# A gated mix of a 2-D spectral filter and a diagonal state space layer: the recurrence re-ordered with chunks outermost, loads released in steps, small work moved between engines

## Chip, cores and metric

The kernel runs on one core of a Trainium2 chip. The metric is device time of one execution in microseconds; the median of three runs of the kernel before is 387.51 us (385.86 to 391.31). Engines are named as in the profile: PE (matmul), PEld (its weight loads), DVE (vector), ACT (scalar), POOL (GpSimd) and SP, which here only issues DMAs. A name with q, such as SPq, is the engine's instruction queue.

## What is computed

`x` has 2048 rows (time) and 1024 columns. Two results are mixed per row by a gate:

```python
X = rfft2(x)                                   # 2048 x 513, complex
a = irfft2(X * (w_r + 1j * w_i)).bfloat16

Lam_bar = exp(exp(log_dt) * Lam)               # 1024 complex states
Bu = einsum("bld,pd->blp", x, B_bar)
h  = Lam_bar * h + Bu[:, t]                    # for each t of 2048
b  = 2 * einsum("blp,dp->bld", h, C).real + x * Dskip

g = sigmoid((x * gate_w).sum(-1))
out = g * a + (1 - g) * b
```

## The kernel before

**Layout.** `big` (16 rows of 1024 per partition) holds the Fourier coefficients, named `FX` with eight planes q, and later a part of C. `xT` is x transposed, `BT` is B transposed in eight blocks jb of 128 states, each with a real and an imaginary half; the three are filled by transposing DMAs that SP issues (L212, L217, L615). `hp` is a pool of eight tiles for h.

**First stage.** x arrives in eight loads `xt`. `fstage` forms sums and differences `eo` on DVE (four elements of each on POOL, L384 to L387), PE transforms them along time (`ps_f`, L398, L399), ACT copies each `ps_f` into two planes of FX (L403). ACT and DVE also work out the small per-state vectors (`scr`, `rho`, `beta`).

**Spectral branch** (`fft_main`). For each of 16 groups g of frequencies: `fd` (PE `ps_d`, ACT copy `X1`, L462), `bf_w` (PE `ps_xe` and `ps_xo`, ACT copies to `X`, then four DVE steps `Y`, `t` that multiply by the weights W, L487 to L490), `bi` (PE `ps_q`, ACT copy back into FX, L514). The matrices `MM` and the weights W are loaded by POOL, two or three groups ahead of need. After group 15 `Gi_sb` is loaded, and for each pair of time residues `idm` (PE `ps_id`, ACT copy `yp`), DVE's `pm` (L582, L583) and `fi` (PE `ps_y`, ACT copies `ya`) follow; SP stores `ya` in DRAM (`ya_scratch`). All `ps_` tiles of this branch share two PSUM buffers.

**State space branch** (`ssm_pair`). The 2048 time steps form four chunks c of 512, the eight state blocks four pairs q; one call does one (c, q), so there are 16, called pairs below. PE makes Bu of the two blocks (`psu`, 32 matmuls of 512 columns, L336), ACT scales it into `u` (L340). DVE rotates it with the tables `tab` (cu, su, cu: L347 to L349, each a pass over 2048 elements), runs four scans (L353), works out the carry into the next chunk in three small steps (L360 to L364), and rotates back into `h` (L367 to L369). `tables(q)` fills the tables of a pair: two ACT passes `xa`, three DVE passes, three ACT sines. `u` has two buffers, so the copy of a pair waits for the pair before the last one to be finished.

**Output** (`gate_pair`, `tile_out`). For each of 16 row tiles tb of 128, DVE multiplies x by the gate weights (`pr`, L672), ACT sums it (L673) and forms the gate `gb`; three small steps (L678 to L682) turn it into the factors `gf` and `om`. DVE scales x by Dskip (L674), ACT scales the stored spectral row (L686). PE forms `psy` (two halves of 17 matmuls: 16 of h with C, L698, and one that adds x, L701), and DVE's `o` (L705) mixes both; SP stores it. `psy` has two buffers.

**Order.** The code is written as generators that are stepped against each other; each yields an estimate of its PE time. SP and POOL keep the order of the program up to the output stage; elsewhere a scheduler places instructions by its own estimates, and the resulting order is fixed before the kernel runs: an engine works its queue in that order and waits where data is missing. The spectral branch runs against `ssm_first` (chunks 0 and 1, with q outermost: both chunks of a pair q one after the other) in the ratio 80 to 58. C arrives in two halves, the first into the first two chunks of xT (L615 by `load_C(0)`), the second into rows 0 to 7 of big (`load_C(1)`). The rows 8 to 15 of big then hold `xc` and `gac` of four row tiles. Chunk 2 runs against the output of chunk 0, with h in a pool of its own (`h2`), chunk 3 against that of chunk 1.

Of the kernel before, what the change touches and what calls it, by code (L numbers as in the profile page):

```python
# [11 lines left out]
ALU = mybir.AluOpType  # L12
# [8 lines left out]
D = 1024  # L21
# [24 lines left out]
def _host_consts():  # L46
# [38 lines left out]
    for b in range(2):  # L85
        kr = 2 * (d + P * b)[:, None]
        ki = kr + 2
        kod = kr + 1
        ck = np.where(kr == 0, 1.0, 2.0)
        Gi[:, 2 * b, 0] = (-ck * np.cos(2 * np.pi * kr * 256 / D))[:, 0]  # L90
        Gi[:, 2 * b, 1:257] = ck * np.cos(2 * np.pi * kr * n0 / D)
        ei = np.zeros((P, 512))
        ei[:, :255] = -2 * np.sin(2 * np.pi * ki * n1[:, :255] / D)
        if b == 1:
            ei[127, :] = 0
            ei[127, 255] = -1.0
            ei[127, 256:] = (-1.0) ** np.arange(256)
        Gi[:, 2 * b + 1, :] = ei
        Gi[:, 4 + 2 * b, :256] = 2 * np.cos(2 * np.pi * kod * n0 / D)
        Gi[:, 5 + 2 * b, :256] = -2 * np.sin(2 * np.pi * kod * n1 / D)  # L100
# [28 lines left out]
GW = [(0, 257), (258, 512), (770, 257), (1028, 255), (1284, 256), (1540, 256), (1796, 256), (2052, 256)]  # L129
GIW = [(0, 257), (258, 255), (514, 257), (772, 512), (1284, 256), (1540, 256), (1796, 256), (2052, 256)]  # L130
GN = 2308
# [10 lines left out]
def kernel(  # L142
# [24 lines left out]
    cG = nc.inline_tensor(_pack(hc["G"], GW), name="c_G").ap()  # L167
    cGi = nc.inline_tensor(_pack(hc["Gi"], GIW), name="c_Gi").ap()
    cMM = nc.inline_tensor(hc["MM"], name="c_MM").ap()
# [158 lines left out]

    def ssm_pair(c, q, hpool):
        u = up.tile([P, 2, 2, TC], BF16, name="u", tag="u")  # L330
# [26 lines left out]
        if c + 1 < NCH:  # L357
            ge = su[:, :, :, TC - 1]
            k1 = sm.tile([P, 2, 2], FP32, name="k1")
            nc.vector.tensor_mul(out=k1, in0=ge, in1=cTC[:, 2 * q:2 * q + 2].unsqueeze(2).to_broadcast([P, 2, 2]))  # L360
            k2 = sm.tile([P, 2, 2], FP32, name="k2")
            nc.vector.tensor_mul(out=k2, in0=ge[:, :, ::-1], in1=sg[:, 2 * q:2 * q + 2, :])
            cy = sm.tile([P, 2, 2], FP32, name=f"carry{q}")
            nc.vector.tensor_add(out=cy, in0=k1, in1=k2)  # L364
            carry[q] = cy
        h = hpool.tile(full, BF16, name="h", tag="h")
        nc.vector.tensor_mul(out=cu, in0=su, in1=tq[:, :, 0:1, ::-1].to_broadcast(full))  # L367
# [8 lines left out]
    def fstage(jj):  # L376
# [15 lines left out]
        for eo_i in range(2):  # L392
            for b in range(2):
                ps = psF.tile([P, 4, 2, P], FP32, name="ps_f", tag="ps")
                bs = slice(P * b, P * (b + 1))
                for jl in range(4):
                    v = eos[jj - 1 + jl // 2][:, jl % 2, eo_i]
                    nc.tensor.matmul(ps[:, jl], lhsT=v[:, 0, bs], rhs=FW_sb[:, 0:2 * P], start=True, stop=False)  # L398
                    nc.tensor.matmul(ps[:, jl], lhsT=v[:, 1, bs], rhs=FW_sb[:, P * (1 + eo_i):P * (3 + eo_i)],  # L399
                                     start=False, stop=True)  # L400
                q = 4 * eo_i + 2 * b
                for r in range(2):
                    nc.scalar.copy(out=FX[:, q + r, :, j0:j0 + 4], in_=ps[:, :, r, :].rearrange("p j c -> p c j"))  # L403
                yield 1.0
# [40 lines left out]
    def fd(g):  # L445
# [16 lines left out]
        nc.scalar.copy(out=X1, in_=ps)  # L462
        X1s[g] = X1

    def bf_w(g):
# [29 lines left out]
    def bi(g):  # L495
        Y = Ys.pop(g)
        M = MM.pop(g)
        Mf = M.rearrange("p a b -> p (a b)")
        nr_, r_, i_, ri_ = Mf[:, 384:512], Mf[:, 512:640], Mf[:, 640:768], Mf[:, 512:768]
        nri = Mf[:, 384:640]  # L500
        ps = psF.tile([P, 8, P], FP32, name="ps_q", tag="ps")
        Yr, Yi = Y[:, 0, :], Y[:, 1, :]
        for b in range(2):
            e = 256 * b
            nc.tensor.matmul(ps[:, 2 * b, :], lhsT=Yr[:, e:e + 255:2], rhs=r_, start=True, stop=False)
            nc.tensor.matmul(ps[:, 2 * b, :], lhsT=Yi[:, e:e + 255:2], rhs=nr_, start=False, stop=True)
            nc.tensor.matmul(ps[:, 2 * b + 1, :], lhsT=Yr[:, e + 2:e + 257:2], rhs=i_, start=True, stop=False)
            nc.tensor.matmul(ps[:, 2 * b + 1, :], lhsT=Yi[:, e + 2:e + 257:2], rhs=r_, start=False, stop=True)
        for b in range(2):
            e = 256 * b + 1  # L510
            dst = ps[:, 4 + 2 * b:6 + 2 * b, :]
            nc.tensor.matmul(dst, lhsT=Yr[:, e:e + 255:2], rhs=ri_, start=True, stop=False)
            nc.tensor.matmul(dst, lhsT=Yi[:, e:e + 255:2], rhs=nri, start=False, stop=True)  # L513
        nc.scalar.copy(out=FX[:, :, 8 * g:8 * g + 8, :], in_=ps.rearrange("p q (c j) -> p q c j", j=16))  # L514

    def idm(j, yp):
        ps = psF.tile([P, 1024], FP32, name="ps_id", tag="ps")

        def mm(q, lo, w, start, stop):
            o, n = GIW[q]  # L520
            nc.tensor.matmul(ps[:, lo:lo + w], lhsT=FX[:, q, :, j], rhs=Gi_sb[:, o:o + w],  # L521
                             start=start, stop=stop, skip_group_check=True)

        mm(3, 0, 512, True, False)
        mm(1, 0, 255, False, False)
        mm(0, 255, 257, False, False)
# [62 lines left out]


    load_BT(0)
    load_xT(0)
    load_BT(1)
    for jj in range(8):
        for _ in fstage(jj):
            pass
        if jj == 5:
            start_consts()
            load_M(0)
            load_W(0)  # L600
    tables(0)
    load_M(1)
    load_W(1)
    load_M(2)
    load_xT(1)
    for jb in range(2, 8):
        load_BT(jb)

    CH = [xT[:, :, 0:1024].rearrange("p j (r d) -> p j r d", r=2), big[:, 0:8].rearrange("p j (r d) -> p j r d", r=2)]

    def load_C(half):
        for dd in range(2):
            for ri, src in enumerate((B_C_re, B_C_im)):
                r0 = 512 * half + 256 * dd
                nc.sync.dma_start_transpose(out=CH[half][:, :, ri, 256 * dd:256 * (dd + 1)], in_=src[r0:r0 + 256, :])  # L615
        nc.vector.tensor_scalar_mul(out=CH[half][:, :, 1, :], in0=CH[half][:, :, 1, :], scalar1=-1.0)

    def ssm_first():
        for q in range(4):
            if q:  # L620
                tables(q)
            for c in range(2):
                yield from ssm_pair(c, q, hp)
            if q == 1:
                load_xT(2)
            if q == 3:
                load_xT(3)
        load_C(0)

# [16 lines left out]

    merge(Gen(fft_main()), Gen(ssm_first()), 80.0, 58.0)
    order1.close()
    fctx.close()

    with ExitStack() as bctx:
        h2 = bctx.enter_context(tc.tile_pool(name="h2", bufs=4))
        fin1 = bctx.enter_context(tc.tile_pool(name="fin1", bufs=1))
        fin = bctx.enter_context(tc.tile_pool(name="fin", bufs=2))
        psY = bctx.enter_context(tc.tile_pool(name="psY", bufs=2, space=PSUM))
        load_C(1)
        gw_bc = fin1.tile([P, D], BF16, name="gw_bc")
# [3 lines left out]

        gates = {}

        def gate_pair(tp):
            gl = fin.tile([P, 2], FP32, name="gl")
            for i in range(2):
                tb = 2 * tp + i
                xc, gac = big[:, 8 + tb % 4, :], big[:, 12 + tb % 4, :]
                nc.sync.dma_start(out=xc, in_=x[P * tb:P * (tb + 1), :])
# [7 lines left out]
            gf = fin.tile([P, 2], FP32, name="gf")  # L677
            nc.vector.tensor_copy(out=gf, in_=gb)  # L678
            ob = fin.tile([P, 2], BF16, name="ob")
            nc.vector.tensor_scalar(out=ob, in0=gb, scalar1=-1.0, scalar2=1.0, op0=ALU.mult, op1=ALU.add)  # L680
            om = fin.tile([P, 2], FP32, name="om")
            nc.vector.tensor_copy(out=om, in_=ob)  # L682
            for i in range(2):
                tb = 2 * tp + i
                gac = big[:, 12 + tb % 4, :]
                nc.scalar.activation(out=gac, in_=gac, func=ACT.Copy, scale=gf[:, i:i + 1])  # L686
                gates[tb] = om[:, i:i + 1]

        def tile_out(tb):
            c, tq = tb // 4, tb % 4  # L690
            xc, gac, om = big[:, 8 + tb % 4, :], big[:, 12 + tb % 4, :], gates[tb]
            psy = psY.tile([P, D], FP32, name="psy")
            for dh in range(2):
                ds = slice(512 * dh, 512 * (dh + 1))
                i = 0
                for jb in range(8):
                    for ri in range(2):
                        nc.tensor.matmul(psy[:, ds], lhsT=hs[c, jb // 2][:, jb % 2, ri, P * tq:P * (tq + 1)],  # L698
                                         rhs=CH[dh][:, jb, ri, :], start=(i == 0), stop=False)
                        i += 1  # L700
# [14 lines left out]

        def b_gen(c, hpool):
            for q in range(4):
                yield from ssm_pair(c, q, hpool)

        def run(g):  # L720
            for _ in g:
                pass

        gate_pair(0)
        bg = Gen(b_gen(2, h2))
        for _ in range(4):
            bg.step()
        merge(Gen(c_gen(0)), bg, 29.0, 24.0)
        merge(Gen(c_gen(1)), Gen(b_gen(3, hp)), 29.0, 29.0)
        run(c_gen(2))  # L730
        run(c_gen(3))


# [28 lines left out]
```

## Time and profile before

| | us |
|---|---|
| median of three runs | 387.51 |
| the profiled execution | 387.79 |
| its span | 386.0 |
| busy: PE, DVE, ACT, POOL | 334.1, 299.0, 197.4, 54.9 |
| all of L353 (64 scans) on DVE | 76.8 |
| all six passes L347 to L349 and L367 to L369 on DVE | 117.0 |
| mean granted PE clock | 0.973 |

The profile is one execution. Its span is the time between the first and the last instruction; 1.8 us of the execution lie outside. Durations of neighbouring instructions overlap by some 0.08 us on DVE and more on PE, since they are pipelined, so a chain of them is best summed by the distance from start to start. A wait is named by what ended it.

### The profile page before, as it was taken

Reading aid. Unit: us, or ns where it says so; the run is one execution under the profiler, and the core shown is the slowest. Engines: PE = TensorE matmul, PEld = TensorE weight load, DVE = VectorE, ACT = ScalarE, POOL = GpSimd, SP = SyncE. Lnnn points to the kernel's source line nnn. Section 1 sums busy time; section 2 is a strip of 40 time slices with the busy share of each in tenths; the row PEclk is TensorE's granted clock in tenths of the full one; section 3 lists DMA queues with packets and bytes.
Section 4 is the critical chain, followed back from the end, with each engine's and each line's share of the span. In section 5 each row is a group of like instructions: output and inputs, shape, how many; then the busy total and the mean of one; then the engine's idle time right before and its main releaser. Section 6 shows DMA issues by size and latency. Waiting matters only on the chain.

```text
span 386.0 us, 4922 instructions
## 1 busy us (share of the span) xinstructions
PE 334.1 (87%) x1794; PEld 176.3 (46%) x1827; DVE 299.0 (77%) x434; ACT 197.4 (51%) x265; POOL 54.9 (14%) x129
## 2 busy tenths in 40 slices
PE   2678969989998897989798389999999997699995
PEld 1554636536554555656343134444444443244442
DVE  3932498999999999986959499399898988984121
ACT  1999846847886767979342077333203132242200
POOL 3680423152534200000000100000000000000000
PEclk9999989989999999999989879999999998999999
DMA  8999993122313110223999704220102022054001
GB/s 302 274 281 226 176 232 83 48 68 73 95 54 91 53 43 19 110 109 101 216 225 226 269 27 139 80 82 16 68 27 82 2 82 82 2 163 136 29 28 53
DMA packets 64520, 43.17 MB, mean 112 GB/s; under 512 B 52928, under 2 KB 53088, under 8 KB 64496
## 3 DMA queue, kind: packets, MB, share of 16 engines
q1 hardware_dynamic: 60544, 33.56, 34.5%
q0 software_dynamic: 3616, 9.13, 8.8%
q8 instruction: 14, 0.23, 0.3%
q10 hardware_dynamic: 336, 0.17, 0.1%
q14 instruction: 10, 0.08, 0.1%
HBM read 21.87 MB, written 8.39 MB: 78 GB/s over the span
## 4 chain that ended last, share of the span: by engine, by line
DVE 43%; PE 25%; ACT 8%; issue 8%; DMA 8%; SPq 6%; POOL 1%; DVEq 0%; ACTq 0%
PE psy L698 16%; DVE su L353 13%; SPq L615 5%; DVE cu L347 3%; DVE su L348 3%; PE psu L336 3%; DVE cu L349 3%; DVE u L368 3%; DMA xt<-in_A_x_dram 3%; DMA MM<-c_MM 3%; DVE o L705 2%; DVE cu L367 2%; ACT u L340 2%; DVE t L488 2%; DMA gw_bc<-in_gate_w_dram 2%
## 5 line engine op out<-in xcount | busy, mean ns | idle before, releaser
L336 PE MATMUL psu<-xT,BT 128*128 128x512 bf16 x490 | 123.0, 387 | 1.2 <-issue 0.2
L698 PEld LDWEIGHTS <-h 128*128 128x128 bf16 x512 | 50.9, 99 | 78.1 <-issue 18.5
L336 PEld LDWEIGHTS <-BT 128*128 128x128 bf16 x512 | 51.0, 100 | 53.1 <-issue 5.5
L698 PE MATMUL psy<-xT,h 128*128 128x512 bf16 x252 | 59.0, 386 | 7.5 <-DVE o L705 5.7
L698 PE MATMUL psy<-big,h 128*128 128x512 bf16 x250 | 58.6, 385 | 0.5 <-issue 0.2
L353 DVE TENSOR_TENSOR_SCAN su<-r_sb,carry,cu 128x512 bf16<-128x512 f32 x48 | 58.1, 1265 | 0.1
L673 ACT ACTIVATE pr<-pr 128x1024 bf16<-128x1024 bf16 x16 | 16.9, 1054 | 80.5 <-DVE pr L672 66.3
L340 ACT ACTIVATE u<-psu,rho 128x1024 bf16<-128x1024 f32 x32 | 35.5, 1112 | 24.9 <-PE psu L336 24.9
L705 DVE SCALAR_TENSOR_TENSOR o<-psy,om,big 128x1024 bf16<-128x1024 f32 x16 | 20.4, 1278 | 24.0 <-PE psy L701 17.9
L347 DVE TENSOR_TENSOR cu<-u,tab 128x2048 bf16<-128x2048 bf16 x16 | 19.5, 1221 | 20.1 <-ACT u L340 20.1
L686 ACT ACTIVATE big<-big,gf 128x1024 bf16<-128x1024 bf16 x16 | 17.5, 1140 | 12.1 <-DVE gf L678 12.1
L398 PE MATMUL ps_f<-BT,eo 128*128 128x256 bf16 x64 | 15.9, 287 | 5.4 <-ACT big L403 5.2
L450 PE MATMUL ps_d<-G_sb,big 128*128 128x256 bf16 (+3 forms) x128 | 19.7, 293 | 0.3
L349 DVE TENSOR_TENSOR cu<-cu,su 128x2048 bf16<-128x2048 bf16 x16 | 19.5, 1221 | 0.3
L514 ACT CAST big<-ps_q 128x1024 bf16<-128x1024 f32 x16 | 16.2, 1012 | 6.9 <-PE ps_q L513 6.8
L369 DVE TENSOR_TENSOR h<-cu,u 128x2048 bf16<-128x2048 bf16 x16 | 19.5, 1218 | 0.2
L367 DVE TENSOR_TENSOR cu<-su,tab 128x2048 bf16<-128x2048 bf16 x16 | 19.5, 1218 | 0.1
L348 DVE TENSOR_TENSOR su<-u,tab 128x2048 bf16<-128x2048 bf16 x16 | 19.5, 1217 | 0.0
L368 DVE TENSOR_TENSOR u<-su,tab 128x2048 bf16<-128x2048 bf16 x16 | 19.5, 1216 | 0.0
L353 DVE TENSOR_TENSOR_SCAN su<-r_sb,cu 128x512 bf16<-128x512 f32 x16 | 18.7, 1209 | 0.1
L487 DVE TENSOR_TENSOR Y<-X,W 128x1028 bf16<-128x1028 bf16 x16 | 10.9, 681 | 9.8 <-ACT X L483 9.8
L521 PE MATMUL ps_id<-Gi_sb,big 128*128 128x256 bf16 (+3 forms) x128 | 17.6, 286 | 0.9 <-DMA Gi_sb<-c_Gi 0.9
(159 smaller groups left out, 495.7 us busy)
## 6 DMA issues: line engine op xcount, KB each, us to landing
xt<-in_A_x_dram SPq DMA_DIRECT2D x8, 512.0 KB, 5.4
ya_scratch<-ya SPq DMA_DIRECT2D x16, 256.0 KB, 2.0
big<-in_A_x_dram SPq DMA_DIRECT2D x16, 256.0 KB, 2.9
big<-ya_scratch SPq DMA_DIRECT2D x16, 256.0 KB, 2.8
out_dram<-o SPq DMA_DIRECT2D x16, 256.0 KB, 2.0
MM<-c_MM POOLq DMA_DIRECT2D x16, 192.0 KB, 2.8
W<-in_A_w_r_dram POOLq DMA_DIRECT2D x31, 64.1 KB, 2.2
W<-in_A_w_i_dram POOLq DMA_DIRECT2D x31, 64.1 KB, 2.2
```

What stands on the lines that cost most here:

```text
L336: nc.tensor.matmul(psu[:, ri, :], lhsT=BT[:, jb, ri, dblk, :], rhs=xT[:, dblk, TC * c:TC * (c + 1)], start=(dblk == 0), stop=(dblk == 7))
L340: nc.scalar.activation(out=u[:, jj], in_=psu, func=ACT.Copy, scale=rho[:, jb:jb + 1])
L347: nc.vector.tensor_mul(out=cu, in0=u, in1=tq[:, :, 0:1, :].to_broadcast(full))
L348: nc.vector.tensor_mul(out=su, in0=u[:, :, ::-1, :], in1=tq[:, :, 1:3, :])
L349: nc.vector.tensor_add(out=cu, in0=cu, in1=su)
L353: nc.vector.tensor_tensor_scan(out=su[:, jj, ri, :], data0=r_sb[:, jb:jb + 1].to_broadcast([P, TC]), data1=cu[:, jj, ri, :], initial=(0.0 ...
L367: nc.vector.tensor_mul(out=cu, in0=su, in1=tq[:, :, 0:1, ::-1].to_broadcast(full))
L368: nc.vector.tensor_mul(out=u, in0=su[:, :, ::-1, :], in1=tq[:, :, 1:3, ::-1])
L369: nc.vector.tensor_add(out=h, in0=cu, in1=u)
L450: nc.tensor.matmul(ps[:, lo:lo + w], lhsT=FX[:, q, 8 * g:8 * g + 8, :], rhs=G_sb[:, o:o + w], start=start, stop=stop, skip_group_check=True)
L698: nc.tensor.matmul(psy[:, ds], lhsT=hs[c, jb // 2][:, jb % 2, ri, P * tq:P * (tq + 1)], rhs=CH[dh][:, jb, ri, :], start=(i == 0), stop=False)
L705: nc.vector.scalar_tensor_tensor(out=o, in0=psy, scalar=om, in1=gac, op0=ALU.mult, op1=ALU.add)
```

## The change

The diff, cut to its core. Line numbers in the prediction are those of the kernel before.

```diff
-        ki = kr + 2
+        ki = kr
...
-        if b == 1:
-            ei[127, :] = 0
-            ei[127, 255] = -1.0
-            ei[127, 256:] = (-1.0) ** np.arange(256)
+        if b == 0:
+            ei[0, :] = 0
+            ei[0, 255] = -1.0
+            ei[0, 256:] = (-1.0) ** np.arange(256)
...
+    def h_tile(c, q):
+        if c != 2:
+            return hp.tile([P, 2, 2, TC], BF16, name="h", tag="h")
+        a, s = 4 * (q % 2), TC * (q // 2)
+        return xT[:, a:a + 4, s:s + TC].rearrange("p (j r) t -> p j r t", r=2)
...
-            nc.vector.tensor_mul(out=k1, in0=ge, in1=cTC[:, 2 * q:2 * q + 2].unsqueeze(2).to_broadcast([P, 2, 2]))
+            nc.gpsimd.tensor_mul(out=k1, in0=ge, in1=cTC[:, 2 * q:2 * q + 2].unsqueeze(2).to_broadcast([P, 2, 2]))
...
-            nc.vector.tensor_mul(out=k2, in0=ge[:, :, ::-1], in1=sg[:, 2 * q:2 * q + 2, :])
+            nc.gpsimd.tensor_mul(out=k2, in0=ge[:, :, ::-1], in1=sg[:, 2 * q:2 * q + 2, :])
...
-            nc.vector.tensor_add(out=cy, in0=k1, in1=k2)
+            nc.gpsimd.tensor_add(out=cy, in0=k1, in1=k2)
...
-                for r in range(2):
-                    nc.scalar.copy(out=FX[:, q + r, :, j0:j0 + 4], in_=ps[:, :, r, :].rearrange("p j c -> p c j"))
+                nc.scalar.copy(out=FX[:, q, :, j0:j0 + 4], in_=ps[:, :, 0, :].rearrange("p j c -> p c j"))
+                nc.vector.tensor_copy(out=FX[:, q + 1, :, j0:j0 + 4], in_=ps[:, :, 1, :].rearrange("p j c -> p c j"))
...
         X1s[g] = X1
+        loads_at(g, X1)
...
-        for b in range(2):
-            e = 256 * b
...
-        for b in range(2):
-            e = 256 * b + 1
...
+        for par in range(2):
+            for b in range(2):
+                e = 256 * b + par
+                dst = ps[:, 4 * par + 2 * b:4 * par + 2 * b + 2, :]
+                nc.tensor.matmul(dst, lhsT=Yr[:, e:e + 255:2], rhs=ri_, start=True, stop=False, **kw)
+                nc.tensor.matmul(dst, lhsT=Yi[:, e:e + 255:2], rhs=nri, start=False, stop=True, **kw)
+        nc.tensor.matmul(ps[0:1, 1, :], lhsT=Yr[:, 512:513], rhs=i_, start=True, stop=False, **kw)
+        nc.tensor.matmul(ps[0:1, 1, :], lhsT=Yi[:, 512:513], rhs=r_, start=False, stop=True, **kw)
...
+    def hold(dst, src):
+        nc.gpsimd.tensor_copy(out=dst, in_=src)
...
-    load_xT(1)
-    for jb in range(2, 8):
-        load_BT(jb)
...
+    def loads_at(g, X1):
+        el = X1[:, 0:1]
+        if g in (0, 2, 4):
+            for jb in (g + 2, g + 3):
+                hold(BT[:, jb, 0, 0, 0:1], el)
+                load_BT(jb)
+        elif g in (5, 11, 14):
+            c = {5: 1, 11: 2, 14: 3}[g]
+            hold(xT[:, 0, TC * c:TC * c + 1], el)
+            load_xT(c)
+    CT = big.rearrange("p (j r) d -> p j r d", r=2)
+    def load_C():
+        for qd in range(4):
+            ds = slice(256 * qd, 256 * (qd + 1))
+            for ri, src in enumerate((B_C_re, B_C_im)):
+                nc.sync.dma_start_transpose(out=CT[:, :, ri, ds], in_=src[ds, :])
+            nc.vector.tensor_scalar_mul(out=CT[:, :, 1, ds], in0=CT[:, :, 1, ds], scalar1=-1.0)
+    def ssm_all():
+        for c in range(NCH):
+            for q in range(4):
+                if c == 0:
+                    tables(q)
+                yield from ssm_pair(c, q)
...
-    merge(Gen(fft_main()), Gen(ssm_first()), 80.0, 58.0)
+    ssm = Gen(ssm_all())
+    fft = Gen(fft_main())
+    while not fft.done:
+        if ssm.t * 80.0 <= fft.t * 46.0:
+            ssm.step()
+        else:
+            fft.step()
...
-                xc, gac = big[:, 8 + tb % 4, :], big[:, 12 + tb % 4, :]
+                xc = fin.tile([P, D], BF16, name="xc", bufs=4)
+                gac = fin.tile([P, D], BF16, name="gac", bufs=4)
...
-            nc.vector.tensor_copy(out=gf, in_=gb)
+            nc.gpsimd.tensor_copy(out=gf, in_=gb)
...
-        bg = Gen(b_gen(2, h2))
-        for _ in range(4):
-            bg.step()
-        merge(Gen(c_gen(0)), bg, 29.0, 24.0)
-        merge(Gen(c_gen(1)), Gen(b_gen(3, hp)), 29.0, 29.0)
-        run(c_gen(2))
-        run(c_gen(3))
+        cg = [Gen(c_gen(c)) for c in range(NCH)]
+        while ssm.t < 8 * 7.2 + 0.0:
+            ssm.step()
+        for c in range(NCH):
+            t0 = ssm.t
+            while not cg[c].done:
+                if not ssm.done and (ssm.t - t0) * 29.0 <= cg[c].t * 29.0:
+                    ssm.step()
+                else:
+                    cg[c].step()
```

In words: all four q of a chunk come before the next chunk, and the spectral branch runs ahead, with fewer pairs beside it (80 to 46). The transposing loads of BT from block 2 on and of xT from chunk 1 on are not issued at once; `loads_at` lets them go at certain groups: POOL copies one element of X1 into the destination, and the load, which overwrites that element, has to wait for it. C is loaded in four quarters of columns into all of big. The h of chunk 2 lies in the columns of xT that held chunks 0 and 1. The odd planes of FX that belong to even frequencies use frequency k instead of k+2, so that the two halves share one 256-column right side; the frequency 512 that is left is computed by two matmuls on one column. The three steps of the carry and the three steps after the gate (`gf`, `ob`, `om`) go to POOL; the second of each two copies of `ps_f` goes to DVE. `xc` and `gac` get four buffers of their own.

## Prediction

> **What bounds the kernel now.** I read the profiled execution (387.79 us, of which 386.0 are span and 1.8 lie around it; the median of the three runs is 387.51, so the sum below also holds for the median within 0.3 us) in this order: busy time by stage, DVE's waits, the timeline of one late pair of state blocks, the timeline of the first stage.
>
> The view of busy time by window, cut at five points: the first DVE step of the recurrence (48.35), the last Y of the frequency stage (141.6), the last ps_id matmul (183.1), the end of the output step o of tile 8 (337.3), the end. Columns: window, its length, then busy us and instructions of PE, PEld, DVE, ACT, POOL, granted clock, DMA share, GB/s.
> ```profile
> 0.00:48.35 48.35, 33.93 (x232) 22.64 (x236) 21.90 (x84) 37.57 (x61) 22.44 (x66) 1.00 1.08 252
> 48.35:141.60 93.25, 82.12 (x541) 48.78 (x549) 91.06 (x129) 65.02 (x77) 30.88 (x60) 0.96 0.35 83
> 141.60:183.10 41.50, 37.97 (x228) 24.47 (x232) 36.29 (x46) 34.62 (x47) 0.54 (x1) 1.00 0.25 87
> 183.10:337.30 154.20, 136.19 (x598) 60.55 (x608) 131.51 (x156) 50.79 (x68) 1.07 (x2) 0.96 0.40 102
> 337.30:386.00 48.70, 43.95 (x200) 19.82 (x203) 18.21 (x24) 9.38 (x14) 0.00 (x0) 1.00 0.24 81
> ```
> I call them A to E. A is ACT's (37.57 busy, without a break from 10 us on). B and most of D are DVE's: 91 of 93 and 131.5 of 154 us. C is shared: ACT 34.6 of 41.5, DVE 36.3. E is pure PE: 200 matmuls that cannot start before o of tile 8 frees its psy buffer. So the end is o(8) plus 48.7 us, and o(8) is where DVE's queue says it is.
>
> DVE's 22 us of idle time in D are listed by the view of waits (who waited for whom, total, times, longest):
> ```profile
> DVE cu L347 <- ACT u L340: 14.7, 6, 4.4
> DVE pr L672 <- DMA gw_bc<-in_gate_w_dram: 4.9, 1, 4.9
> DVE pr L672 <- DMA big<-in_A_x_dram: 1.4, 1, 1.4
> ```
> The first row comes from ACT's order, as the timeline of one pair shows (start, length, engine and line):
> ```profile
> 289.92 1.23 DVE L369 TENSOR_TENSOR h<-cu,u 128x2048 bf16<-128x2048 bf16 x1
> 291.06 1.28 DVE L705 SCALAR_TENSOR_TENSOR o<-psy,om,big 128x1024 bf16<-128x1024 f32 x1
> 292.26 0.68 DVE L672 TENSOR_TENSOR pr<-big,gw_bc 128x1024 bf16<-128x1024 bf16 x1
> 292.97 0.69 DVE L674 TENSOR_TENSOR big<-big,dsk_bc 128x1024 bf16<-128x1024 bf16 x1
> 295.21 1.22 DVE L347 TENSOR_TENSOR cu<-u,tab 128x2048 bf16<-128x2048 bf16 x1 [1.55 <-ACT u L340]
> ```
> ACT's sum over pr waits for DVE's pr, and u of the next pair stands behind it on ACT, so DVE waits 1.5 us for u. One pair (cu, su, cu, four scans, cu, u, h) takes 279.03 to 291.06, 12.03 us; o takes 1.2 more, pr and xc 0.7 each.
>
> **The change, stage by stage.** PE's matmuls for Bu and for the output, and the DVE passes of 16 pairs, stay as they are in number. What moves is how many pairs lie before the last ps_id: in the built order the changed kernel has issued 232 of the 512 psu matmuls by then, the old one 260. On DVE that is 6 pairs and the start of a seventh, against 7 and the start of an eighth.
>
> Stage A. FX's evacuation is halved: 16 of 32 ACT copies of 0.53 us (6.42 us for 12) leave ACT, 8.3 us. They become 16 DVE copies from PSUM of 512 elements; the nearest row is L705, 1.28 us for 1024, so 0.62 to 0.65 each, 10 us. DVE needs, from the arrival of vps at 7.3 us: 30 eo steps spaced 0.36 (10.8), 42 small steps (3.9, the rest of 7.3 to 23.6 less its 1.6 of waits), 10 of copies, 2.5 of xa: 34.5 to 36 us. Old ACT released the first X1 at 37.7. So ACT's 8 us turn into a DVE bound about as late; but the first pair's psu is complete earlier in PE's order (ahead of the first ps_q instead of two groups later), and u of its second half stands before that ps_q copy on ACT. I take 46.0 for the first cu, from 44 (ACT's gain half kept) to 51 (DVE copies at the whole 1.28).
>
> In A too: the BT transposes past block 1 and chunk 1 to 3 of xT now wait on SP for POOL copies that wait for X1 of groups 0, 2, 4, 5, 11, 14. Queued behind them on SP are only other transposes and, much later, the ya stores; on POOL the W and MM loads. Each W load stands behind a Y step that comes later than that X1, so nothing on POOL is late by it. BT 2 and 3 are let go at 37.7; four issues of 1.31 us and 5.5 us of landing bring them by 49, and PE's order first reads them (33rd psu) at about 44, block 2's first half only, landed by then. Cost 0, at most 3 us of PE in B, where DVE has 16 us of Y and pair 1 ahead of it. What it can win: MM of group 3 landed 7.26 us after its issue at 47.08, against a median of 2.8, while the old BT and xT transposes ran; but DVE idled only 2.1 and 1.9 us in B, so the gain is 0 to 4. I take none.
>
> Stage B. Between first cu and last Y the new DVE order holds 26 passes of 2048, 16 scans, 3 table sets and the Y work, the old one 31, 20, 2 and 5 carries. At the spacing of this stage (1.135 a pass, 1.14 to 1.19 a scan, 2.35 a table set, 0.08 a small step) that is 5.7 + 5.0 + 1.2 - 2.4 = 9.5 less; 0.6 of Y comes in. 91.3 becomes 82.4. Idle: old 4, new 5.6, since the second table set puts three ACT passes of 1.05 before the u that pair 2 needs. B = 88. ACT carries about 80 us in it, 56 for the FFT copies.
>
> The k=512 edit lies here: ps_q took eight matmuls of 128 columns spaced 0.055 and four of 256 spaced 0.11, 0.88 us; now eight of 256 and two of 128, 0.99. 16 x 0.11 = 1.8 us of PE, covered by PE's wait for Y (5.5 us before ps_q in all); uncovered it costs 1.8.
>
> Stage C. Gi lands 4.5 us after the last Y and eight double steps follow. Old: ps_y on PE waited three times for DVE's pm, which stood between the passes of pairs 6 to 8; 5.1 us a step. New: DVE has 28 us of work here, so ACT paces: two yp of 1.0, four ya of 0.5, a third of a u, 4.4 us; six steps at 4.6 instead of 5.1. C = 38.5, taken 38 (35 to 41.5).
>
> Stage D. Against the old 154.2: one pair more, 12.0; o(8) now stands behind the last pair's cu, u, h, 3.5; carry and gate steps leave DVE, 30 x 0.08 = 2.3; the old idle 22 goes. New idle: C's eight transposes all start after the last ps_id (2.3 to 2.7 us each on SP, the old ones did so from 185.9 on as well), with ya stores between them; the sign flips stand in DVE's queue between pair 8's steps, and by 2.5 us a transpose and 5 of landing DVE waits 2.2, 0.9 and 0.5 for them. PE meanwhile has 39 psu and a half tile. After each pr, ACT still holds up u: with sum 1.15, u 1.0, and for every second pair gb and two gate passes (2.2), against h and xc (1.75) or cu, u, xc, h (4.1) of cover on DVE, it comes to 1.1, 0.5, 1.1, 0.5, 3.4, so 6.6. Other 2. D = 154.2 + 12.0 + 3.5 - 2.3 - 22 + 12.2 = 157.6, taken 158 (148 to 164). Loads of xc and gac keep depth four; h of chunk 2 in xT removes no wait that DVE shows: 0.
>
> Carry and gate steps on POOL: a carry is needed three pairs later, some 40 us. The gate is needed by ACT's gac pass. The timeline of A, on the two engines:
> ```profile
> 5.67 0.20 POOL L384 TENSOR_TENSOR eo<-xt 128x2 bf16<-128x2 bf16 x1
> ...
> 11.78 0.39 POOL L384 TENSOR_TENSOR eo<-xt 128x2 bf16<-128x2 bf16 x1
> ...
> 11.69 0.41 DVE L379 TENSOR_TENSOR eo<-xt 128x512 bf16<-128x512 bf16 x1
> 12.02 0.41 DVE L380 TENSOR_TENSOR eo<-xt 128x512 bf16<-128x512 bf16 x1
> 12.36 0.41 DVE L381 TENSOR_TENSOR eo<-xt 128x510 bf16<-128x510 bf16 x1
> ```
> POOL's step takes 0.20 us with DVE idle and 0.39 beside DVE's eo steps, while those stay spaced 0.33 to 0.34, as they are at 22 us where POOL only issues DMAs. So POOL is late by at most one DVE pass (1.2 us) and DVE pays 0; the other end is POOL's 0.20 for each of the 54 steps that lie before o(8), 10.8 us.
> The Trainium skill, SBUF — State Buffer, Who interferes with whom, says that a DVE step with two SBUF inputs and a GpSimd step that reads SBUF lock each other out for the whole instruction, whichever starts first. By it DVE would have to stand still whenever POOL's step starts first, and the sum would be up to 391; the rows show only POOL waiting, which gives 380.5.
>
> Stage E: 12 half tiles of 3.67 and 4.7 to the end, 48.7 as before.
>
> Sum: 46 + 88 + 38 + 158 + 48.7 = 378.7 span, 380.5 with the 1.8.
>
> **Rivals.** (1) DVE keeps saturated: the sign flips find their data and u is always ready. For it: PE and ACT have slack in D. Against: ACT's order. B 85, C 35, D 148: 46 + 85 + 35 + 148 + 48.7 + 1.8 = 364.5; half of it, 370. (2) Slower: ACT becomes the bound of B and C. It has 80 us in 88 and each table set waits for DVE in the middle of it; if its waits exceed 8 us, B and C stay at 93.3 and 41.5 while D still carries the extra pair: 46 + 93.3 + 41.5 + 158 + 48.7 + 1.8 = 389.3. It decides when ACT's FFT copies start late on more than every third group. (3) POOL blocks DVE by the 0.20 of each of its 54 steps: 391. (4) The release does not spread the transposes, or starves PE: 3 us more, 384.
>
> **Numbers.** Forecast 0.50 (own range 374 to 388), rival 1 0.22, rival 2 0.17, rival 3 0.06, rival 4 0.05. Two per cent, about what a measurement of this kernel tells from no change, is 379.8 below and 395.3 above. Below lie 0.45 of the forecast and all of rival 1, 0.45; above it the tails of 2 and 3 (D at 164, A at 51), 0.11. The range 367 to 392 leaves out a fifth.
>
> **What would show it.** First cu near 46; last ps_id near 172; o(8) ending near 330; about 49 us of PE alone after it. The step h of chunk 2 (L369 before) at the length of the others, and POOL's carries on no chain. Wrong if the last ps_id lies at 180 or later (rival 2), if DVE passes beside POOL steps are spaced over 1.3 us (rival 3), or if DVE's idle time from the last ps_id to o(8) is under 6 us (rival 1) or over 18.

## The result and the profile after

The changed kernel takes 406.45 us (median of 4 runs, 402.14 to 408.43) against 386.69 of the kernel before in the same batch (4 runs, 385.0 to 391.31): a ratio of 1.0489, 95% interval 1.0371 to 1.0607. It is about 20 us slower, where 380.5 was forecast and 367 to 392 was the range. Executions of one kernel fall into a faster and a slower group; ratios and intervals are taken from the faster runs, while medians and ranges are of all runs. The profiled execution is 406.74 us with a span of 405.0.

Busy time by window, cut at the same five events as before (first cu, last Y, last ps_id, end of o of tile 8, end). Columns as before: window, length, busy us and instructions of PE, PEld, DVE, ACT, POOL, granted clock, DMA share, GB/s.
```profile
0.00:45.44 45.44, 32.41 (x213) 21.19 (x217) 29.77 (x97) 28.56 (x43) 20.45 (x64) 1.00 0.76 202
45.44:154.47 109.03, 85.17 (x509) 49.16 (x516) 82.61 (x111) 67.97 (x81) 59.77 (x84) 0.91 0.53 108
154.47:194.65 40.18, 37.02 (x222) 23.77 (x225) 35.79 (x39) 30.71 (x43) 13.33 (x7) 1.00 0.24 91
194.65:354.46 159.81, 143.44 (x623) 63.51 (x635) 139.96 (x135) 52.05 (x71) 36.13 (x38) 0.96 0.35 91
354.46:405.00 50.54, 45.67 (x200) 20.28 (x203) 14.35 (x16) 10.34 (x16) 1.04 (x6) 0.95 0.23 79
```
Against the forecast of 46, 88, 38, 158 and 48.7 the stages miss by -0.6, +21.0, +2.2, +1.8 and +1.8: 26.3 us in all, and 21.0 of them in B. DVE's work in B is what was forecast (82.61 busy, 82.4 forecast); what is new is that DVE stands idle for 26 of 109 us. No engine fills the stage any more. POOL, which had 30.9 us there, has 59.8.

Who waited for whom, PE in B (total, times, longest):
```profile
PE ps_xe L479 <- DMA MM<-c_MM: 20.2, 4, 8.3
```
The same row of the kernel before:
```profile
PE ps_xe L473 <- DMA MM<-c_MM: 3.6, 2, 3.0
```
The page's groups of instructions name the other end (busy us, mean ns, then idle time before it and its releaser):
```profile
L365 POOL TENSOR_TENSOR k<-su,snc 128x4 f32<-128x4 bf16 x12 | 47.6, 3967 | 78.3 <-DVE su L358 78.3
...
L702 ACT ACTIVATE gac<-gac,gf 128x1024 bf16<-128x1024 bf16 x16 | 17.5, 1140 | 13.0 <-POOL gf L694 13.0
...
L479 PE MATMUL ps_xe<-X,MM 128*128 128x256 bf16 x16 | 4.7, 296 | 20.9 <-DMA MM<-c_MM 20.2
```
The first carry step works on four elements per partition and takes 3.97 us on average. The timeline (DVE and POOL alone) shows what it does in that time, at its longest, and once where it is short:
```profile
114.01 0.67 DVE L493 TENSOR_TENSOR Y<-X,W 128x1028 bf16<-128x1028 bf16 x1
114.18 9.46 POOL L365 TENSOR_TENSOR k<-su,snc 128x4 f32<-128x4 bf16 x1 [3.45 <-DVE su L358]
114.60 1.22 DVE L372 TENSOR_TENSOR cu<-su,tab 128x2048 bf16<-128x2048 bf16 x1
115.73 1.22 DVE L373 TENSOR_TENSOR u<-su,tab 128x2048 bf16<-128x2048 bf16 x1
116.87 0.69 DVE L494 TENSOR_TENSOR t<-X,W 128x1028 bf16<-128x1028 bf16 x1
...
123.17 0.42 DVE L496 TENSOR_TENSOR Y<-Y,t 128x514 bf16<-128x514 bf16 x1
123.59 0.19 POOL L367 TENSOR_TENSOR k<-su,sg 128x4 f32<-128x4 bf16 x1
123.86 0.20 POOL L369 TENSOR_TENSOR carry<-k,k 128x4 f32<-128x4 f32 x1
124.35 0.51 POOL L439 DMA_DIRECT2D W<-in_A_w_r_dram  x1 [0.29 <-issue]
124.57 1.23 DVE L352 TENSOR_TENSOR cu<-u,tab 128x2048 bf16<-128x2048 bf16 x1 [0.98 <-ACT tab L320]
...
126.32 0.62 POOL L432 DMA_DIRECT2D MM<-c_MM  x1
...
236.48 1.26 DVE L721 SCALAR_TENSOR_TENSOR o<-psy,om,gac 128x1024 bf16<-128x1024 f32 x1
236.91 0.20 POOL L365 TENSOR_TENSOR k<-su,snc 128x4 f32<-128x4 bf16 x1
```
POOL starts at 114.18 and ends at 123.64, just after DVE's queue has its first gap (123.59 to 124.57). In between DVE runs fourteen steps, each beginning before the last has ended, and its passes of 2048 elements are spaced 1.13 and 1.14 us, as in the kernel before: DVE pays nothing, POOL gets nowhere. With the gap there, the next two carry steps take 0.19 and 0.20. Behind them on POOL's queue stand a W load and the MM load, which goes out at 126.32; without the held step it would be some 9 us earlier, by an estimate from the 9.46 us. Beside o, which reads its large operand from PSUM, the same step takes 0.20. The chain of waits runs over the same places, with shares of the span:
```profile
DVE 33%; PE 23%; issue 14%; POOL 10%; ACT 7%; DMA 6%; SPq 5%; DVEq 0%; POOLq 0%; ACTq 0%
```
and two of its pieces are 114.18 (9.46 us, POOL's k) and 126.32 (2.69 us, the landing of that MM load).

In D, the row that answers to DVE's 14.7 us of waits for u:
```profile
DVE cu L352 <- ACT u L345: 18.6, 6, 6.6
```
and the timeline of one such wait:
```profile
318.70 0.69 DVE L688 TENSOR_TENSOR pr<-xc,gw_bc 128x1024 bf16<-128x1024 bf16 x1
...
319.48 1.06 ACT L689 ACTIVATE pr<-pr 128x1024 bf16<-128x1024 bf16 x1 [9.17 <-DVE pr L688]
...
320.66 0.20 ACT L692 ACTIVATE gb<-gl 128x2 bf16<-128x2 f32 x1
...
321.20 2.19 ACT L702 ACTIVATE gac<-gac,gf 128x1024 bf16<-128x1024 bf16 x2 [0.34 <-POOL gf L694]
...
323.30 2.09 ACT L345 ACTIVATE u<-psu,rho 128x1024 bf16<-128x1024 f32 x2
324.42 1.22 DVE L352 TENSOR_TENSOR cu<-u,tab 128x2048 bf16<-128x2048 bf16 x1 [3.30 <-ACT u L345]
```
The order pr, sum, gb, gac, u on ACT is the one that the forecast counted for every second pair, with 3.4 us; it is 3.3 here.

### The profile page after: what moved, and what is told of

It is laid out like the page before. It is cut to its first block, busy times and chain, and to the rows that moved or that the text cites. A ratio compares the mean times of both kernels' runs of the same rounds, so it can differ in the third digit from the quotient of the medians.

```text
span 405.0 us, 4879 instructions
## 1 busy us (share of the span) xinstructions
PE 343.7 (85%) x1762; PEld 177.9 (44%) x1795; DVE 302.5 (75%) x392; ACT 189.6 (47%) x249; POOL 130.7 (32%) x198
## 4 chain that ended last, share of the span: by engine, by line
DVE 33%; PE 23%; issue 14%; POOL 10%; ACT 7%; DMA 6%; SPq 5%; DVEq 0%; POOLq 0%; ACTq 0%
DVE su L358 11%; PE psy L714 11%; POOL k L365 6%; PE psu L341 5%; SPq L629 4%; DMA MM<-c_MM 3%; DMA xt<-in_A_x_dram 2%; DVE cu L352 2%; DVE su L353 2%; DVE o L721 2%; DVE cu L372 2%; DVE u L373 2%; DVE cu L354 2%; ACT u L345 2%; PE ps_id L525 1%
## 5 line engine op out<-in xcount | busy, mean ns | idle before, releaser
L714 PE MATMUL psy<-big,h 128*128 128x512 bf16 x376 | 89.0, 387 | 0.4
L341 PEld LDWEIGHTS <-BT 128*128 128x128 bf16 x512 | 51.2, 101 | 59.8 <-issue 12.0
L365 POOL TENSOR_TENSOR k<-su,snc 128x4 f32<-128x4 bf16 x12 | 47.6, 3967 | 78.3 <-DVE su L358 78.3
L714 PEld LDWEIGHTS <-h 128*128 128x128 bf16 x384 | 38.3, 100 | 51.6 <-issue 8.1
L721 DVE SCALAR_TENSOR_TENSOR o<-psy,om,gac 128x1024 bf16<-128x1024 f32 x16 | 20.4, 1275 | 28.0 <-PE psy L717 28.0
L694 POOL CAST gf<-gb 128x2 f32<-128x2 bf16 x8 | 7.4, 930 | 91.0 <-ACT gb L692 91.0
L714 PE MATMUL psy<-big,xT 128*128 128x512 bf16 x125 | 30.5, 395 | 4.4 <-DVE o L721 4.3
L702 ACT ACTIVATE gac<-gac,gf 128x1024 bf16<-128x1024 bf16 x16 | 17.5, 1140 | 13.0 <-POOL gf L694 13.0
L518 ACT CAST big<-ps_q 128x1024 bf16<-128x1024 f32 x16 | 16.3, 1020 | 15.2 <-PE ps_q L517 15.1
L479 PE MATMUL ps_xe<-X,MM 128*128 128x256 bf16 x16 | 4.7, 296 | 20.9 <-DMA MM<-c_MM 20.2
L714 PEld LDWEIGHTS <-xT 128*128 128x128 bf16 x128 | 13.0, 101 | 21.0 <-issue 7.0
L483 ACT CAST X<-ps_xe 128x514 bf16<-128x514 f32 x16 | 12.0, 752 | 20.2 <-PE ps_xe L482 18.3
```

Source lines behind the costliest of these rows:

```text
L341: nc.tensor.matmul(psu[:, ri, :], lhsT=BT[:, jb, ri, dblk, :], rhs=xT[:, dblk, TC * c:TC * (c + 1)], start=(dblk == 0), stop=(dblk == 7))
L365: nc.gpsimd.tensor_mul(out=k1, in0=ge, in1=cTC[:, 2 * q:2 * q + 2].unsqueeze(2).to_broadcast([P, 2, 2]))
L721: nc.vector.scalar_tensor_tensor(out=o, in0=psy, scalar=om, in1=gac, op0=ALU.mult, op1=ALU.add)
```

## The experiments

My theory after the result: POOL's small steps that read SBUF are shut out while DVE runs one SBUF step after the other, and the cost is what is queued behind them on POOL, the W and MM loads. The rivals: the late carry itself is on the path; the release of the loads costs (its hold copies sit on POOL, and the transposes run between PE's groups); the new order costs. "B less waits" below is the length of B less PE's waits for MM. Medians of different rows come from different batches, each with its own runs of the kernel before; across rows, compare the ratios.

| kernel | median us (runs) | ratio to before, 95% | B, us | PE's waits for MM | B less waits |
|---|---|---|---|---|---|
| changed kernel | 406.45 (4) | 1.0489, 1.0371 to 1.0607 | 109.0 | 20.2 | 88.8 |
| e1: carry on DVE | 396.92 (4) | 1.0197, 1.0114 to 1.028 | 94.2 | 7.7 | 86.5 |
| e2: carry, gate on DVE | 393.4 (4) | 1.0122, 1.001 to 1.0234 | 94.3 | 7.1 | 87.2 |
| e3: release at once | 410.69 (4) | 1.06, 1.0517 to 1.0684 | 109.7 | 21.5 | 88.2 |
| e4: e2 and e3 | 391.52 (10) | 1.0085, 1.0034 to 1.0135 | 92.1 | 4.3 | 87.8 |
| e8: e3, loads by SP | 397.49 (4) | 1.0256, 1.0187 to 1.0325 | 95.8 | 8.4 | 87.4 |
| e10: e4, FX on ACT | 394.75 (4) | 1.0168, 1.0113 to 1.0222 | 94.3 | 7.6 | 86.7 |
| e12: e10, no flips | 393.36 (4) | 1.0113, 1.0068 to 1.0159 | 92.1 | 5.2 | 86.9 |
| e14: e4, no flips, MM early | 387.54 (10) | 0.997, 0.9915 to 1.0026 | 90.5 | 1.2 | 89.3 |
| e15: changed, MM early | 402.0 (4) | 1.0337, 1.0267 to 1.0408 | 98.5 | 10.4 | 88.1 |

**e1 and e2: the small steps back on DVE.**
e1 moves the steps k1, k2 and cy from POOL to DVE, e2 the steps gf, ob and om as well.
```diff
-            nc.gpsimd.tensor_add(out=cy, in0=k1, in1=k2)
+            nc.vector.tensor_add(out=cy, in0=k1, in1=k2)
...
-            nc.gpsimd.tensor_copy(out=gf, in_=gb)
+            nc.vector.tensor_copy(out=gf, in_=gb)
```


> The changed kernel with only the three carry steps back on DVE. Theory 1 (POOL's carry step starves beside back-to-back DVE work and holds up the loads of W and MM that are queued behind it on POOL): the last Y falls from 154.5 us to 140 or earlier, PE's wait for MM from 20 us to under 10, time 384 to 392. Theory 2 (the order itself, chunks outermost, costs the time): within 3 us of 406. Theory 3 (the releases of the transposes cost it): within 3 us of 406 as well.

> The same, and the three gate steps back on DVE as well. Theory 1 with the same starvation for the gate: ACT's 13 us of waits for the factor gf shrink, 3 to 6 us less than the kernel with the carries alone moved back. If the gate steps find gaps on DVE anyway: within 2 us of it.

With the carry on DVE the ratio falls from 1.0489 to 1.0197, and the intervals do not meet: 0.029 of 387 is 11 us. B shortens by 15 us. The gate steps bring a lower median, 393.4 after 396.92, but the intervals overlap; that is not settled. ACT's waits for gf, which moving the gate steps back was expected to shorten, are 13.0 us in the changed kernel, 9.2 in e1 and 10.0 in e2, and were 12.1 in the kernel before: the gate steps on POOL are not shown to cost anything.

**e3: releases undone, carry still on POOL.** The loads of BT and of xT's chunk 1 are issued at once, chunks 2 and 3 without a hold.

> The changed kernel with its carries on POOL, but without the held loads: BT 2 to 7 and chunk 1 of xT are issued at once, chunks 2 and 3 of xT at their places without a hold. Theory 1: within 3 us of 406. Theory 3: 8 us or more below it, PE's first wait for MM (8.3 us) gone.

The time is not better without the release (1.06 against 1.0489, overlapping), and PE waits as long for MM (21.5). The release is not what costs beside a blocked POOL.

**e6: the kernel before with the three carry steps on POOL, nothing else.**

> The kernel before with nothing but the three carry steps moved to POOL. Theory 1: the loads behind them on POOL come late here as well, and the second chunk of a pair follows the first directly, so its scans also wait: 398 or more. Theories 2 and 3: 384 to 389, as DVE loses 2 us of work.

402.65 us (4 runs, 401.11 to 404.11), ratio 1.0375, 1.0309 to 1.044. PE waits 18.8 us for MM, against 3.6, and B takes 106.3 us, against 93.3. This one edit of three lines loses some 14 us in the old order too.

**e7: does reading matter?** The kernel before, with a memset and a copy of four elements on POOL behind each carry, in alternating order.
```diff
+            nc.gpsimd.memset(k1, 0.0)
+            nc.gpsimd.tensor_copy(out=k2, in_=cy)
```


> The kernel before with two more POOL steps of four elements behind each carry: a memset that only writes, and a copy that reads and writes SBUF; their order alternates from pair to pair. If what holds POOL up is any access of POOL beside DVE's two-input steps, memset and copy both take from 1 us to over 5 us in some of their 12 instances. If it is the read alone, every memset takes under 0.6 us and only copies take longer. If POOL merely starts late whatever it does, the first of the two is long and the second short, whichever it is.

Groups of instructions of e7:
```profile
L371 POOL COPY k<-carry 128x4 f32<-128x4 f32 x12 | 45.9, 3825 | 83.3 <-DVE carry L364 83.3
...
L368 POOL MEMSET k<- 128x4 f32 x12 | 1.2, 99 | 49.9 <-DVE carry L364 49.9
```
and its timeline, one instance of each order:
```profile
79.84 0.10 POOL L368 MEMSET k<- 128x4 f32 x1 [6.26 <-DVE carry L364]
79.89 6.44 POOL L371 COPY k<-carry 128x4 f32<-128x4 f32 x1
...
125.17 6.41 POOL L371 COPY k<-carry 128x4 f32<-128x4 f32 x1 [5.20 <-DVE carry L364]
131.53 0.09 POOL L368 MEMSET k<- 128x4 f32 x1
```
All twelve memsets take 0.09 to 0.10 us, inside the same stretch of DVE steps in which the copies take 1.02 to 7.59. The step that reads SBUF is shut out, the one that only writes is not. Nothing needs the result of these copies, and the kernel still takes 401.98 us (one run), with 17.7 us of PE's waits for MM in B: what costs is the queue behind.

**e8: another queue for the loads.** e3 with the MM loads from group 3 and the W loads from group 2 on issued by SP.
```diff
-        nc.gpsimd.dma_start(out=m, in_=cMM[g])
+        (nc.gpsimd if g < 3 else nc.sync).dma_start(out=m, in_=cMM[g])
```


> e3_release_at_once (410.7) with the MM and W loads from group 3 and 2 on issued by SP and not by POOL; carry and gate steps stay on POOL. If the cost of the carry steps is that these loads are queued behind them, the carries still take up to 9 us, PE's waits for MM fall from 21.5 us to under 6, and the time falls by 10 us or more, to 396 to 400. If the late carry itself is on the path (the next chunk's scan waits for it), PE's waits for MM do not matter and it stays at 408 to 412.

Waits of PE in B of e8, then its group of the first carry step:
```profile
PE ps_xe L480 <- DMA MM<-c_MM: 8.4, 2, 7.8
```
```profile
L365 POOL TENSOR_TENSOR k<-su,snc 128x4 f32<-128x4 bf16 x12 | 54.1, 4507 | 146.7 <-DVE su L358 146.7
```
The carry steps are held up even longer (54.1 us), and the kernel is 13 us faster than e3. The late carry itself costs little; the loads behind it cost. The waits fall to 8.4, not below 6 as expected: one MM load of 7.8 remains, on a queue that also issues the transposes. The Trainium skill, SBUF — State Buffer, Who interferes with whom, puts a DMA of POOL's that stalls beside DVE down to its descriptors, for which POOL then gets no port time, and the cure is another queue; it adds that its probe saw this beside tensor_copy and not beside tensor_tensor, the kind of step that cu and su are. The cure works here. The reason does not show: POOL's issues take 0.51 to 0.62 us beside DVE's cu and su at 124.57 and 125.71, and the loads were late because they had not been issued.

**e4: both undone, small steps and release.**

> The changed kernel with carry and gate steps on DVE and the transposing loads let go at once; beside e2_carry_gate_on_dve (393.4) it differs by the release alone. If the release is what is left of the loss (in e2 PE still waited 7.1 us for MM in stage B, while the transposes ran between its groups), these waits go and the time is 386 to 389. If the release is a gain also with a free POOL, as e3 against the changed kernel has it (4 us), it is 396 to 399. If it is nothing, 392 to 395.

391.52 us, between the first and the third case; its interval overlaps that of e2. With POOL free the release is worth nothing, or costs a little. Stages of e4: 45.1, 92.1, 41.7, 158.3, 50.1.

**e9 and e10: FX's copies alone.** e9 is the kernel before with the second copy of each ps_f on DVE; e10 is e4 with it back on ACT.

> The kernel before with one edit: the second copy of each ps_f goes to DVE. By the working of stage A the first cu comes 2.3 to 3 us earlier; since DVE's queue sets the end, all of it shows: 384 to 386. The rival: the 10 us that DVE takes over lie partly behind the first cu, in a stage that DVE fills (91 of 93 us), and the time is 388 to 391.

> e4_dve_smalls_release_at_once (391.5) with both copies of each ps_f back on ACT. The 16 copies are 0.68 us each on DVE, 10.9 us of DVE that the kernel before did not have. If this DVE work is what is left of the loss (e9 put the split alone on the kernel before and lost about 5), the time is 385 to 388, although the first cu comes 2 to 3 us later. If the split only fills time in which DVE waits in stage A, undoing it moves the first cu back and the time is 393 to 395.

e9: 394.26 us (4 runs: 390.45, 391.17, 397.35, 397.85), where the kernel before had 387.64 (13 runs, 384.39 to 395.2); no ratio is on record, and on its two lower runs a loss is likely but not settled. In the profiled execution (390.45) the first cu is 2.3 us earlier, as worked out, and B takes 98.2 instead of 93.3. The rival had the longer B, but for another reason: the last copy ends at 37.2, ahead of the first cu, so none of this work lies in B. There DVE is busy 92.9 us after 91.1, and idle 5.3 after 2.2; why was not looked into. In the new order the split is a gain: undoing it moves the first cu from 45.1 to 49.0 and the ratio from 1.0085 (e4) to 1.0168 (e10), where the intervals just overlap. The pair without the sign flips, described next, settles it: 1.0012 (e11) to 1.0113 (e12, split undone), in one batch and with intervals that do not meet, some 4 us.

**e11, e12, e13: no sign flips.** In e4 DVE waits 9.8 us for C_im before the flips. The scans of the imaginary halves subtract, so that the conjugate of h comes out, and C needs no flip.
```diff
-                                             op0=ALU.mult, op1=ALU.add)
+                                             op0=ALU.mult, op1=ALU.subtract if ri else ALU.add)
...
-        nc.vector.tensor_mul(out=u, in0=su[:, :, ::-1, :], in1=tq[:, :, 1:3, ::-1])
+        nc.vector.tensor_mul(out=u, in0=su[:, :, ::-1, :], in1=tq[:, :, 2:0:-1, ::-1])
...
-            nc.vector.tensor_scalar_mul(out=CT[:, :, 1, ds], in0=CT[:, :, 1, ds], scalar1=-1.0)
```


> e4_dve_smalls_release_at_once without DVE's sign flips of C: the scans of the imaginary halves subtract in place of adding, so that the conjugate of h comes out, and the sign pair of the back rotation and of the carry is swapped; the sum is the same. The DVE waits 9.8 us for C_im in front of the flips and spends 2.8 us on them. If these waits are part of the loss, DVE's idle time in stage D falls by 6 us or more and the time is 381 to 386. If the wait only moves (PE needs the same C for psy, o then waits for psy), it is 389 to 392.

> Both edits of e10 and e11 on e4. If the losses are separate, the gains add up: 376 to 382. If both remove the same idle time of DVE, it stands where the better of the two stands.

> The kernel before with the edit of e11. There the first flips wait 0.3 us in all, and DVE spends 2 steps of about 1.2 us on them. If the waits for C are a cost of loading C in one go after the last ps_id, as only the changed kernel does, this brings 2 to 3 us here: 384 to 386. If the edit itself is worth more than the waits, it brings 6 or more: below 382.

e11: 390.75 us (10 runs), ratio 1.0012, 0.9968 to 1.0055; e12 is in the table; e13: 389.68 (10 runs), 1.0032, 0.9987 to 1.0077, no different from before. DVE's waits in D, of e4 and then of e12:
```profile
DVE cu L352 <- ACT u L345: 9.9, 5, 3.0
DVE big L626 <- DMA big<-in_B_C_im_dram: 9.8, 3, 6.0
```
```profile
DVE cu L352 <- ACT u L345: 16.4, 5, 9.5
DVE pr L683 <- DMA xc<-in_A_x_dram: 4.8, 1, 4.8
```
The wait for C is gone, and u and xc (0.3 in e4) take over 11.0 of the 12.6 us that the flips (2.8) and their waits held. The expected 6 us did not come; 2 to 3 us did, at the edge of what the intervals tell.

**e14, e15, e16: the MM load one W load earlier.** A fourth MM buffer, and the load at the head of its group.
```diff
-            bi(g)
-            if g + 3 < 16:
-                load_M(g + 3)
+            bi(g)
```


> e11_e4_no_flips (390.8) with each MM load issued one W load earlier on POOL (a fourth MM buffer, the load at the head of its group). In e4 one MM came 3.1 us late and DVE waited 4.8 us for the u behind it in stage B. If stage B's 92 us against the forecast of 88 are these late loads, PE's waits for MM go below 1 us, B shortens by 3 to 5 us and the time is 385 to 388. If B is held by the order of PE and ACT whatever the loads do, it is 389 to 392.

> The changed kernel as it is, carry and gate steps on POOL, with MM loads one W load earlier as in e14. If the cost of the carries is what stands behind them on POOL's queue, a part of PE's 20 us of waits for MM turns into slack, and the time falls from 406 to 395 to 401, while the carries still take up to 9 us. If the carry itself is what is late, it stays at 404 to 408.

> e13_before_no_flips (389.7, as the kernel before) with MM loads one W load earlier. PE waits 3.6 us for MM in the kernel before, DVE 4 us in all in stage B: at most 3 us are to be had, 385 to 389. If a kernel faster than the one before is to be had from these edits, this is it; if DVE's queue is what fills stage B, nothing changes: 387 to 390.

e15 leaves all the small steps on POOL, where the first carry step takes 51.8 us in all, more than in the changed kernel, and halves PE's waits for MM: B is 10.5 us shorter; 402.0 us is a little above what was expected, and its interval still touches that of the changed kernel. Of the 10.5 us, 5 reach the end in the profiled execution (span 400.0 after 405.0): C takes 44.5 us there and D 161.4. e14 takes the waits to 1.2 us and is the best kernel with the new order: 0.997 of before, the same within its interval. Six of its ten runs lie at 385.34 to 387.61, three at 394.02 to 396.25 and one at 883.41, which nothing on record explains. e16 is no gain on the kernel before: 390.78 us (10 runs), 1.0102, 1.0043 to 1.0161, although PE no longer waits for MM at all there; DVE's built order differs, and B took 95.3. Why was not looked into. How much it lost is unclear: the medians of all runs in this batch are 390.78 and 389.58. No version beat the kernel before by more than the measurement tells.

## Why the prediction was wrong, step by step

**The step that failed** is what was drawn, for the carry and gate steps, from the timeline of A: "POOL is late by at most one DVE pass (1.2 us) and DVE pays 0". The second half was right: DVE's passes keep their spacing of 1.13 to 1.14 us. The first half rested on rows of A, 0.20 us alone and 0.39 beside DVE's eo steps of 0.41 us. There POOL's step began 0.09 us after a DVE step had begun, and it ended with it, although these DVE steps too follow one another without a gap. In B the long ones began 0.15 us or more after the start of a DVE step, and every further DVE step that began before the last had ended kept POOL out: up to 9.46 us, the time of eight passes. The row was from the wrong stage: it showed one way in which the two can meet, and not the other. Whether the moment of the start alone decides was not tried by an edit.

**And the price was asked of the wrong party.** "a carry is needed three pairs later, some 40 us" is true and was no help. What was needed sooner was the rest of POOL's queue: "nothing on POOL is late by it" was said of the hold copies, and the carries were never followed to the loads behind them. An MM load is for a group three later, and a group takes some 6 us (93 us for the 16 in B), but that lead was used up before the change. In the kernel before, the MM of group 3 and of the twelve after it landed only 0 to 4.2 us ahead of its first use; the one of group 9, for example, is issued at 94.49, and PE's weight load is waiting when it lands:
```profile
94.49 0.60 POOL L427 DMA_DIRECT2D MM<-c_MM  x1
...
97.28 0.10 PEld L473 LDWEIGHTS <-MM 128*128 128x128 bf16 x1 [0.46 <-DMA MM<-c_MM]
```
So most of a delay of 4 to 9 us had to reach PE. In e14, where the load goes out one W load earlier, the same slack is 3.7 to 8.6 us from group 5 on. Rival 3 had a price for POOL's steps, 0.20 us for each of 54, as a block on DVE; the block fell on POOL, and through its queue on PE.

**How much of the miss this is.** e2, which only puts the small steps back on DVE, has a span of 389.8 us in its profiled execution: 15.2 of the 26.3 us are gone. The 11.1 that stay lie in B (94.3, +6.3, with 7.1 us of waits for MM), C (41.7, +3.7) and D (159.6, +1.6), less 0.7 in A; they belong to other terms, which follow below.

The rule that was weighed there, from the Trainium skill, SBUF — State Buffer, Who interferes with whom, has the two lock each other out for a whole instruction, the first to start winning. On POOL's side the runs fit the lock, and its condition that the GpSimd step reads SBUF (e7: 0.10 against up to 7.59 us). The other side of the rule, DVE waiting while POOL's step runs, shows only as 0.03 us: where POOL's step began 0.02 us ahead of DVE's pass (at 276.52 in the changed kernel), POOL took its 0.19 us and the pass 1.25 instead of 1.22. "Whole instruction" is too short: the step that lost once kept losing, over fourteen instructions.

**B itself** was right but for that. B less PE's waits for MM is 86.5 to 89.3 us in all ten kernels of the table, and 88 was forecast. The waits add to it nearly one for one, from 1.2 to 21.5 us. This agreement over the runs is what ties the 21 us to the MM loads; e6, e8 and e15 show the causes of these waits by changing one thing each. In the old order it holds less well: 89.7 in the kernel before, 87.5 in e6 and 88.9 in e13, but 92.8 in e9 and 95.3 in e16. Of the forecast's parts, DVE's work was right (82.61 us for 82.4), though its four scans fewer make 4.8 us and not 5.0; its idle time was 26.4 instead of 5.6.

**A**: 45.4 for 46. DVE's last FX copy ended at 36.6 us, close to the 34.5 to 36 that was worked out (a copy takes 0.68 us, not 0.62 to 0.65); then DVE waited 5.3 us for ACT's X. Kernels with the same first stage had their first cu between 45.1 and 48.2, and e11 at 53.3 in its profiled execution of 394.04 us.

**C**: 40.2 for 38. DVE has 35.8 us of work in it, not 28; 140.0 in D, not 145.8. The split of pairs between C and D was mis-sized (26 of the 64 scans, six and a half pairs, lie ahead of the last ps_id), so that DVE has more to do in C than ACT (35.8 us against 30.7) and fills it in e4 (40.7 busy of 41.7).

**D**: 159.8 for 158, with two errors that nearly cancel. 5.8 us of DVE's work lay ahead of D, and its idle time there was 19.9 instead of 12.2. That is over the 18 that the prediction set as its own bound. u is the reason (18.6 us of waits against 6.6); the flips' waits, forecast at 3.6, are 0.2 in the changed kernel and 9.8 in e4.

**E**: 50.5 for 48.7. PE is busy 45.67 us with the same 200 matmuls for which the kernel before took 43.95; the granted clock is 0.95 there, and was 1.00.

**The rivals.** Rival 1 (DVE saturated) is refuted: idle time grew in B, and D's did not fall under 6 us. Rival 2 (ACT bounds B and C) has the right side, and the last ps_id late, but not the mechanism: ACT is busy 68 of 109 us in B, where the prediction had 80. In rival 1, half of its gain would be 372.5 and not 370; nothing else rests on that. Rival 4 (the release) is refuted as the cause by e3. h of chunk 2 in dead columns of xT cost nothing (1.22 us a step, as the others). The k=512 edit was not tried alone. One rival was not named ahead: the granted clock in B is 0.91, after 0.96. PE is busy 85.2 us there with 509 matmuls, and 82.3 in e2 with 521 at 0.98; that is about 3 us of busy time, in a stage in which PE stands idle for 24, and cannot be the 21.

**What the change is worth without the fault**: nothing that these runs show. e2, the change with its small steps back on DVE, stands at 1.0122 of the kernel before (1.001 to 1.0234), e4, which also undoes the release, at 1.0085 (1.0034 to 1.0135). e14 reaches 0.997, with two edits that the change does not have (no flips, MM early). The forecast saw 7.3 us in the span: 2.4 in A, 5.3 in B, 3.5 in C, less 3.8 in D. e14's stages are 48.2, 90.5, 41.7, 156.1 and 48.8, a span of 385.4 against 386.0: B gives half of what it was to give, C nothing, A nothing in this execution, and D takes 1.9.

## What to carry to other kernels

Before a small step moves to POOL, look at what DVE does in that stretch: where DVE works without a gap on operands in SBUF, a POOL step that reads SBUF can wait for all of it. Then follow POOL's queue past the moved step: DMA issues behind it are late by the same time, and here they, not the step's own result, set the price. Look in the trace at how long before its first use each of these loads lands; the number of buffers does not tell. Take the price of a step from a row in the stage to which it moves, not from a quieter one.

## What the runs showed of the hardware

- POOL's steps on four elements took 0.19 to 0.20 us in gaps and beside o, which reads PSUM, and up to 9.46 us beside DVE's SBUF steps in the changed kernel (11.86 in e15). A memset of four elements took 0.09 to 0.10 us in all twelve cases of e7.
- Of the twelve first carry steps of the changed kernel, the seven long ones (4.23 to 9.46 us) began 0.15 us or more after the start of a DVE step, and ended where DVE had a gap, even one of 0.03 us (DVE's next step waiting for its predecessor's result). Three began within 0.05 us of the start of a pass and ended with that pass, 1.23 or 1.24 us later; carry steps that began 0.09 or 0.10 us after the start of a pass took 1.18. Why these got in was not tried, and the line between the two is not sharp: a hold copy that began at 0.11 us took 2.96.
- Beside DVE's scans a POOL step took up to 1.2 us, about one scan, and no more.
